# Seven half-width products per pair of feature tiles in a two-layer FFN behind delta-rule attention

## The chip, the cores and the metric

One core of a Trainium2 chip runs the whole program. The time is the device time of one launch in microseconds (us), as the median of several executions. PE is TensorE, DVE VectorE, ACT ScalarE, SP SyncE, which issues the DMAs.

## What is computed

Attention by the delta rule over 4 batches, 8 heads, 768 positions of 48 numbers, then two feed-forward layers over the 3072 tokens of 384 numbers, all in float32:

```
k_n = k / (norm(k) + 1e-06)
for t in range(S):                       # state: 48x48 for each batch and head
    y[:, :, t] = einsum('bhd,bhde->bhe', q[:, :, t], state)
    v_old = einsum('bhde,bhd->bhe', state, k_n[:, :, t])
    state = state + beta_t * einsum('bhd,bhe->bhde', k_n[:, :, t], v_t - v_old)
x = y.transpose(0, 2, 1, 3).reshape(3072, 384)
h = x @ moe_w_in                         # 384 -> 2048
x = maximum(0.01 * h, h) @ moe_w_out     # 2048 -> 384
h = x @ moe2_w_in
out = (h - tanh(h)) @ moe2_w_out
```

## The kernel before

**Tiling.** The positions are cut into 12 chunks n of 64; with four batches a chunk is 256 tokens. Two chunks make one of six pairs u in the attention (`keys`, `grams`, `inverses`, `merges`, then for each chunk `queries`, `products`, `states`, `outputs`). `to_xa` scales a chunk's attention output and turns it, and makes of it the input of the first layer, i = 0; `to_xb` does the same between the first layer and the second, i = 1.

**The layers.** Each float32 product is made of three products of float16: of a high half and a low half of either operand, all but low by low. The 2048 features are 16 tiles in 8 pairs. `h_part` makes a pair's hidden values: 18 products with a block of the first weight (WI) as the stationary operand and 256 columns of x moving, into one bank of ps_h. ACT applies the function (tile sx), ACT copies the high half in float16 (g) and DVE subtracts it for the low half (g again; "g<-sx,g"). `o_part` then takes g as the stationary operand, in blocks of 128 tokens, and the second weight (WO) as the moving one: 12 products of 384 columns per pair, in two banks of ps_o that collect all eight pairs of a chunk. In the program's first moments, PE also measures the two first weights with products of 128 columns ("ps_h<-wi", "ps_o<-wo"). `layer` runs `h_part` for the eight pairs and lets `o_part` follow LAG = 3 pairs later; `layers` gives the order of chunks, two at a time: (0,0) (1,0) (0,1) (1,1) (2,0) and so on.

**Weights.** They arrive as words of float64 in rooms that are free at the time. DVE turns them into float32 (one TENSOR_SCALAR and two SCALAR_TENSOR_TENSOR per two tiles, "wi<-wo,wi"), and they are then scaled and split ("wo<-wo,sw,sx" is the low half of a tile pair of weight 1, the first layer's WO). Weight 3, the second layer's WO, lands in the freed parts of others and in two rooms of x.

**Rooms.** Tiles live in rings: x has 4 rooms, sx 6, g LAG + 1 = 4, kf (keys) 4, kt 3, q, gd and vf 2; in PSUM ps_h and ps_o 2 banks each, ps_a 4, which the attention uses. A tile waits until its room's last reader is done.

**The order.** Nothing is issued as it is written. Every operation is recorded in a `Graph`, with what it reads and writes; a list scheduler then puts all in one order for each engine, by the length of what hangs on an operation plus a number for its stage from the table `BIAS` (some 300 numbers). The engines issue in that order. So all instructions of the trace have the same line, that of the helper: L631 for PE and L634 for the others. Names tell them apart; a name's number is its room.

## Time and profile before

| | |
|---|---|
| median of 3 runs | 954.79 us (954.46 to 954.85) |
| the profiled execution | 953.02 us |
| its span in the trace | 951.3 us |
| PE busy | 898.3 us (94%), 13194 products |
| weight loads (PEld), beside it | 684.2 us (72%) |
| DVE busy | 596.4 us (63%), 1334 instructions |
| ACT busy | 492.2 us (52%), 1193 instructions |
| first products (ps_h, 256 columns) | 3456, 403.7 us of busy time |
| second products (ps_o, 384 columns) | 2304, 400.3 us of busy time |

How to read it: 1.7 us of the profiled execution's time lie outside its span. Busy times are shares of one execution; records of products run into each other, so the mean of one tells less than the distance from start to start in a row of them.

### The profile page before, as it was taken

How to read it: one execution, taken by the hardware profiler on the slowest of the kernel's cores; microseconds unless marked ns; L12 is line 12 of the kernel's file. 1: busy time of each engine (PE TensorE's matmuls, PEld its weight loads, DVE VectorE, ACT ScalarE, POOL GpSimd, SP SyncE). 2: the span in 40 equal slices, each digit the busy share in tenths (PEclk: the TensorE clock that was granted, in tenths of full speed). 3: DMA queues.
4: the chain of work that ended last, by engine and by line, in shares of the span. 5: the costliest groups of instructions: out<-in, count | busy, mean ns of one | idle time of the engine just before them, and what ended most of it. 6: DMA issues, size and time to landing. Idle time of an engine off the chain costs nothing.

```text
span 951.3 us, 29839 instructions
## 1 busy us (share of the span) xinstructions
PE 898.3 (94%) x13194; PEld 684.2 (72%) x13194; DVE 596.4 (63%) x1334; ACT 492.2 (52%) x1193; POOL 4.9 (1%) x22
## 2 busy tenths in 40 slices
PE   3087999999999999999999999999999999999997
PEld 3056877777778778777877777777777777777775
DVE  7999999996984337983598353266943344312432
ACT  5266957976735435735564654354334543434432
POOL 2000000000000000000000000000000000000000
PEclk9587899999999999999999999999999999999999
DMA  9964535643230302222122150031200010000000
GB/s 350 400 209 125 177 99 167 151 133 60 69 60 11 70 22 58 81 45 31 41 58 53 41 94 4 17 57 36 57 1 19 2 36 18 18 18 17 18 17 18
DMA packets 82498, 70.32 MB, mean 74 GB/s; under 512 B 57536, under 2 KB 68800, under 8 KB 82368
## 3 DMA queue, kind: packets, MB, share of 16 engines
q1 hardware_dynamic: 82368, 68.41, 27.1%
q8 instruction: 103, 1.69, 0.7%
q14 instruction: 27, 0.22, 0.1%
HBM read 44.14 MB, written 4.72 MB: 51 GB/s over the span
## 4 chain that ended last, share of the span: by engine, by line
PE 84%; DVE 10%; ACT 3%; DMA 1%; issue 1%; SPq 1%; ACTq 0%; DVEq 0%
PE ps_h L631 38%; PE ps_o L631 38%; PE ps_a L631 8%; DVE wo L634 2%; DVE wi L634 2%; DVE xi L634 2%; DVE gd L634 2%; ACT sx L634 1%; DMA kf<-in_k_dram 1%; SPq L634 1%; ACT jk L634 0%; ACT XW L634 0%; DVE sx L634 0%; ACT gd L634 0%; DVE p L634 0%
## 5 line engine op out<-in xcount | busy, mean ns | idle before, releaser
L631 PE MATMUL ps_h<-x,wi 128*128 128x256 f16 x3456 | 403.7, 273 | 0.3 <-DVE sx L634 0.3
L631 PE MATMUL ps_o<-wo,g 128*128 128x384 f16 x2304 | 400.3, 326 | 0.0
L631 PEld LDWEIGHTS <-wi 128*128 128x128 f16 (+1 forms) x3504 | 340.2, 98 | 77.5 <-DVE wi L634 22.9
L631 PEld LDWEIGHTS <-g 128*128 128x128 f16 x2304 | 222.5, 98 | 133.0 <-DVE g L634 0.2
L634 ACT ACTIVATE g<-sx 128x512 f16<-128x512 f32 x192 | 120.4, 628 | 97.3 <-DVE sx L634 50.0
L634 DVE TENSOR_TENSOR g<-sx,g 128x512 f16<-128x512 f32 x96 | 66.2, 690 | 108.7 <-ACT g L634 108.4
L634 ACT ACTIVATE sx<-ps_h 128x512 f32<-128x512 f32 x96 | 56.9, 595 | 136.6 <-PE ps_h L631 112.3
L634 DVE SCALAR_TENSOR_TENSOR g<-sx,g 128x512 f16<-128x512 f32 x96 | 66.2, 690 | 63.3 <-ACT g L634 62.9
L634 DVE SCALAR_TENSOR_TENSOR sx<-sx,kap,ps_h 128x512 f32<-128x512 f32 x96 | 71.4, 744 | 54.0 <-ACT sx L634 53.8
L634 ACT ACTIVATE sx<-ps_h,kap 128x512 f32<-128x512 f32 x96 | 65.3, 680 | 33.5 <-PE ps_h L631 21.0
L634 DVE TENSOR_TENSOR gd<-xi 128x30 f32<-128x30 f32 (+9 forms) x180 | 59.6, 331 | 2.6
L634 DVE TENSOR_TENSOR xi<-xi,gd 128x30 f32<-128x30 f32 (+9 forms) x180 | 59.7, 332 | 2.3
L634 ACT ACTIVATE jk<-kf 128x48 bf16<-128x48 f32 x160 | 38.3, 239 | 20.3 <-DMA kf<-in_k_dram 17.0
L634 ACT ACTIVATE sx<-x,sxs 128x384 f16<-128x384 f32 (+1 forms) x36 | 25.5, 715 | 13.6 <-DVE sxs L634 11.3
L634 ACT ACTIVATE gd<-ps_a 32x256 f32<-32x256 f32 (+1 forms) x72 | 23.6, 372 | 15.5 <-PE ps_a L631 15.0
L634 DVE SCALAR_TENSOR_TENSOR wi<-wo,wi 128x768 int32<-128x768 int32 x32 | 30.3, 956 | 0.0
L634 ACT ACTIVATION_READ_ACCUMULATOR jk<-kf 128x1 f32 x160 | 30.0, 188 | 0.0
L634 DVE SCALAR_TENSOR_TENSOR sx<-x,sxs,sx 128x384 f16<-128x384 f32 (+1 forms) x36 | 26.9, 749 | 4.2 <-ACT sx L634 4.1
L631 PE MATMUL ps_h<-wi 128*128 128x128 bf16 x48 | 4.6, 284 | 22.7 <-DVE wi L634 22.7
L634 DVE TENSOR_SCALAR sx<-ps_o,kap 128x384 f32<-128x384 f32 x12 | 7.4, 616 | 29.7 <-PE ps_o L631 29.7
L634 ACT ACTIVATE sx<-x 128x384 bf16<-128x384 f32 (+1 forms) x36 | 22.3, 621 | 6.2 <-DVE x L634 3.8
L634 ACT ACTIVATE x<-ps_o,sxs 128x384 f32<-128x384 f32 x23 | 12.6, 579 | 21.4 <-PE ps_o L631 21.3
(129 smaller groups left out, 742.1 us busy)
## 6 DMA issues: line engine op xcount, KB each, us to landing
wo<-in_w_in_dram SPq DMA_DIRECT2D x32, 384.0 KB, 7.9
q<-in_q_dram SPq DMA_DIRECT2D x12, 512.0 KB, 4.2
wi<-in_w_out_dram SPq DMA_DIRECT2D x14, 384.0 KB, 7.7
kf<-in_k_dram SPq DMA_DIRECT2D x12, 384.0 KB, 3.6
vf<-in_v_dram SPq DMA_DIRECT2D x12, 384.0 KB, 3.4
out_dram<-sx SPq DMA_DIRECT2D x48, 96.0 KB, 2.2
x<-in_w_out_dram SPq DMA_DIRECT2D x10, 384.0 KB, 4.3
b<-in_beta_dram SPq DMA_DIRECT2D x6, 512.0 KB, 4.8
```

Of the source, the lines that this page charges most:

```text
L631: self.eng["pe"].matmul(out=o.real(), lhsT=lhsT.real(), rhs=rhs.real(), start=start, stop=stop)
L634: getattr(self.eng[n.on], op)(**{k: v.real() if isinstance(v, View) else v for k, v in kw.items()})
```

## The change

For the chunks from the fifth on (`STRA = 4`), the first layer's second product is made of seven products per pair of feature tiles where a two-by-two scheme has eight: the two halves of the tokens and the two tiles of the pair make a 2x2 array of blocks of g, and the two tiles and the two halves of the output columns a 2x2 array of blocks of WO. The seven products take single blocks or sums and differences of blocks, and each still is three products of float16: 21 products of 192 columns in place of 12 of 384. They collect in four PSUM banks, two of ps_o and two of ps_a, over the chunk's eight pairs.

What comes with it:
- `h_part` makes seven blocks of g in float16 halves in place of four: three more sums on DVE, one more copy on ACT and one more subtraction on DVE, one more room of sx. A room of g grows from 512 to 896.
- `to_xb` gathers a chunk's output from the four banks with four ACT copies and eight DVE steps of 128x3x64, where there were two copies.
- `kept_sums` and `differences` prepare the sums of blocks of the weight, once, ahead of chunk 4. They lie in one room each of q, gd, kt, kf and vf and in a fixed tile, so that these rings have one room less from then on. Blocks of WO are overwritten with differences, after which only the new scheme can use them.
- `layers` takes the first layer of the first four chunks in a row, then their second layer, then pairs as before.
- Weight 3 lands in two rooms of the keys (kf) at u = 2, and no longer in rooms of x.
- The scale of weights 0 and 1 is 2**14 in place of 2**15, so that sums have room.
- `BIAS` is a new table for all stages, so the order on every engine is new. Lines move by seven: L638 for PE, L641 for the others.

```diff
@@ -30,9 +30,11 @@
 def layers(n):
-    out = []
-    for u in range(n // 2):
-        out += [(2 * u, 0), (2 * u + 1, 0), (2 * u, 1), (2 * u + 1, 1)]
+    out, c = [], 0
+    while c < n:
+        w = 2 if c else FIRST
+        out += [(c + j, i) for i in range(2) for j in range(w)]
+        c += w
@@ -55,95 +57,100 @@
 TURNS = 2
+STRA = 4
+LAG = 3
+FIRST = 4
+W3_AT = 2
+WS = (("q", 2, 1), ("gd", 2, 1), ("kt", 2, 1), ("kf", 2, 0), ("vf", 0, 4), ("", 0, 1))
 BIAS = {
-    ('consts', 0): 156.13, ('dma', 'b', 0): 45.42, ('dma', 'b', 1): -53.35, ('dma', 'grams', 10): 13.82,
...
+    ('consts', 0): -120.49, ('diffs', 0): 58.69, ('diffs', 1): 84.59, ('diffs', 2): 88.56,
...
@@ -667,7 +674,6 @@
     NP = NF // 2
-    LAG = 3
@@ -683,7 +689,7 @@
     s_r = ring("sx", SROOMS, 512, short=True)
-    g_r = ring("g", LAG + 1, 512)
+    g_r = ring("g", LAG + 1, 512 if STRA >= NS else 896)
@@ -914,7 +920,7 @@
             dve("tensor_reduce", out=acc[:, 0:1], in_=diag, axis=AX.X, op=ALU.add)
-        pow2_scale(s_, norm_sum(acc, 1 if trace else NF), 2 ** 15)
+        pow2_scale(s_, norm_sum(acc, 1 if trace else NF), 2 ** (15 if i > 1 or STRA >= NS else 14))
@@ -1048,6 +1054,10 @@
                 turn(land[c_].rearrange("p (m i) -> p m i", m=GM), KH[:, c_].rearrange("p m g d -> p (m g d)"))
+                if c_ == 0:
+                    g_.claim(g_.nodes[-1], kt)
+                    if n % 2 == 0 and STRA < NS:
+                        g_.claim(g_.nodes[-1], gd_t[n // 2])
@@ -1074,7 +1084,7 @@
             for t in (Gd, raw_t.get(n // 2)):
-                if t is not None:
+                if t is not None and not (n in K_DMA and STRA < NS):
@@ -1366,6 +1376,57 @@
+    WH = WO[0].rearrange("p f c (t h e) -> p f c h t e", t=KT, h=2)
+    HD2 = DM // 2
+    R, G = [], []
+
+    def te(v):
+        return v.rearrange("p (t e) -> p t e", t=KT)
+
+    def fte(v):
+        return v.rearrange("p f (t e) -> p f t e", t=KT)
+
+    def pair_sum(outs, shape, a, b, op, view):
+
+        s, l = (g_.tile(s_r, shape, F32) for c in range(2))
+        tt(view(s), a[1], b[1], op)
+        g_.claim(g_.nodes[-1], l)
+        for part, o in outs:
+            copy(o[1], part(s))
+        tt(view(l), a[0], b[0], op)
+        tt(l, l, s, ALU.add)
+        for part, o in outs:
+            tt(o[0], part(l), o[1], ALU.subtract)
+
+    def kept_sums():
+        for r, pairs, n in WS:
+            w = 4 * pairs * HD2 + 2 * n * HD2
+            t = g_.tile(dict(q=q_r, gd=gd_r, kt=kt_r, vf=vf_r, kf=kf_r, x=x_r)[r], [128, w], F16) if r else fixed(f"ws{n}", [128, w], F16)
+            for c in range(pairs):
+                R.append(t[:, 4 * HD2 * c:4 * HD2 * c + 4 * HD2].rearrange("p (c f e) -> p c f e", c=2, f=2))
+            for c in range(n):
+                o = 4 * pairs * HD2 + 2 * c * HD2
+                G.append(t[:, o:o + 2 * HD2].rearrange("p (c e) -> p c e", c=2))
+        for p in range(NP):
+            g_.stage = "sums", p // 2
+            f = slice(2 * p, 2 * p + 2)
+            pair_sum([(fte, [fte(R[p][:, c]) for c in range(2)])], [128, 2, HD2], [WH[:, f, c, 0] for c in range(2)],
+                     [WH[:, f, c, 1] for c in range(2)], ALU.add, fte)
+            pair_sum([(te, [te(G[p][:, c]) for c in range(2)])], [128, HD2], [WH[:, 2 * p, c, 0] for c in range(2)],
+                     [WH[:, 2 * p + 1, c, 1] for c in range(2)], ALU.add, te)
+
+    def differences():
+        def half_of(h):
+            return lambda v: v.rearrange("p (t h e) -> p h t e", t=KT, h=2)[:, h]
+
+        for p in range(NP):
+            g_.stage = "diffs", p // 2
+            pair_sum([(half_of(h), [WH[:, 2 * p + 1 - h, c, h] for c in range(2)]) for h in range(2)], [128, DM],
+                     [WO[0][:, 2 * p, c] for c in range(2)], [WO[0][:, 2 * p + 1, c] for c in range(2)], ALU.subtract,
+                     lambda v: v)
+
+
+
@@ -1433,14 +1494,29 @@
         x = g_.tile(x_r, [128, KT * N], F32)
-        for k in range(HB2):
-            cp(rows_of(x)[:, k], po[k][:, 0:DM].rearrange("p (t f) -> p t f", t=KT), sx[:, 2 + k:3 + k])
+        if n < STRA:
+            for k in range(HB2):
+                cp(rows_of(x)[:, k], po[k][:, 0:DM].rearrange("p (t f) -> p t f", t=KT), sx[:, 2 + k:3 + k])
+        else:
+            xr = x.rearrange("p (t k h e) -> p k h t e", t=KT, k=HB2, h=2)
+
+            def gather(k, h, m, *rest):
+                o, sc = xr[:, k, h], sx[:, 2 + k:3 + k]
+                copy(o, product(po, m), sc)
+                for m, op in rest:
+                    stt(o, product(po, m), sc, o, ALU.mult, op)
+
+            gather(0, 0, 4, (2, ALU.subtract))
+            gather(1, 0, 4, (5, ALU.add), (1, ALU.subtract), (7, ALU.add))
+            gather(0, 1, 2, (6, ALU.add), (1, ALU.subtract), (3, ALU.add))
+            gather(1, 1, 3, (5, ALU.add))
         g_.stage = f"h_part{i}", n
+        seven = i == 0 and n >= STRA
@@ -1451,7 +1527,7 @@
         sx = g_.tile(s_r, [128, 2 * N], F32)
-        g = g_.tile(g_r, [128, 2, 2 * N], F16)
+        g = g_.tile(g_r, [128, 2, 7, 128] if seven else [128, 2, 2 * N], F16)
@@ -1459,7 +1535,18 @@
             stt(sx, sx, kap[:, 1:2], ps, ALU.mult, ALU.add)
-        if i == 0:
+        if seven:
+            rs = g_.tile(s_r, [128, 4, 128], F32)
+            g_.claim(node, rs)
+            sq = sx.rearrange("p (j o m) -> p j o m", j=2, o=2)
+            tt(rs[:, 0:2], sq[:, 0], sq[:, 1], ALU.add)
+            tt(rs[:, 2:4], sq[:, :, 1], sq[:, :, 0], ALU.subtract)
+            tt(sq[:, 1, 1], sq[:, 0, 1], sq[:, 1, 0], ALU.add)
+            sq = sx.rearrange("p (q m) -> p q m", q=4)
+            for a, b, src in ((0, 3, sq[:, 1:4]), (3, 7, rs)):
+                copy(g[:, 0, a:b], src)
+                tt(g[:, 1, a:b], src, g[:, 0, a:b], ALU.subtract)
+        elif i == 0:
@@ -1480,6 +1567,29 @@
             g_.ffn(node)
+
+    SEVEN = {4: (0, 0, 1), 2: (0, 1, 3), 1: (1, 0, 2), 5: (1, 1, 4), 3: (2, 0, 0), 6: (2, 1, 5), 7: (3, 0, 6)}
+
+    def product(po, m):
+        b, c, _ = SEVEN[m]
+        return te(po[b][:, c * HD2:c * HD2 + HD2])
+
+    def o_seven(n, po, g, p):
+        g_.stage = "o_part0", n
+
+        e, o = 2 * p, 2 * p + 1
+        w = {1: lambda c: te(G[p][:, c]), 2: lambda c: WH[:, e, c, 0], 3: lambda c: WH[:, e, c, 1],
+             4: lambda c: WH[:, o, c, 0], 5: lambda c: WH[:, o, c, 1], 6: lambda c: te(R[p][:, c, 0]),
+             7: lambda c: te(R[p][:, c, 1])}
+        for m, (b_, c_, q_) in SEVEN.items():
+            if c_ == 0:
+                g_.cut()
+            for n, (a, b) in enumerate(((0, 0), (0, 1), (1, 0))):
+                node = mm(product(po, m), g[:, b, q_], w[m](1 - a), p == 0 and c_ == 0 and n == 0,
+                          p == NP - 1 and n == 2 and (c_ == 1 or m == 7))
+            if c_ or m == 7:
+                g_.ffn(node)
+
@@ -1501,9 +1611,14 @@
             po += [g_.tile(ps_o, [128, 512], F32) for o in range(2)]
+            if i == 0 and n >= STRA:
+                po += [g_.tile(ps_a, [128, 512], F32) for o in range(2)]
             out_scale(kap)
-        o_part(n, i, po, g, p)
+        if i == 0 and n >= STRA:
+            o_seven(n, po, g, p)
+        else:
+            o_part(n, i, po, g, p)
@@ -1552,9 +1667,12 @@
     weight(2, w2_in, WI2[1], (wo[1] * 2)[0:NF])
-    xw = [words(g_.tile(x_r, [128, 2 * DM], F32))[0] for _ in range(2)]
-    weight(3, w2_out, WO[1], (wo[1][nh // 2:] * 2)[0:NF // 2] + xw * (NF // 4))
     for u in range(NU):
+        if u == W3_AT:
+            xw = [words(g_.tile(kf_r if u else x_r, [128, 2 * DM], F32))[0] for _ in range(2)]
+            weight(3, w2_out, WO[1], (wo[1][nh // 2:] * 2)[0:NF // 2] + xw * (NF // 4))
+        if 2 * u == STRA:
+            kept_sums()
@@ -1573,6 +1691,8 @@
     for n, i in layers(NS):
+        if n == STRA and i == 0:
+            differences()
```

The table's numbers tell nothing to the eye; the orders that come of them do. The first place is DVE around the input of chunk 0: the second "sx<-x,sxs,sx" makes the low half of it, "xi" and "gd" are steps of the solving in `inverses`, "wi" is a conversion of weight 2, and "wo" a scaling of weight 1. Before:

```order
L634 SCALAR_TENSOR_TENSOR wi_130<-wo_132,wi_130 128x768
L634 COPY x_62<-ps_a_99 128x3x128
L634 SCALAR_TENSOR_TENSOR sx_66<-x_61,sxs_113,sx_65 128x3x128
L634 COPY u_87<-ps_a_98 128x384
L634 TENSOR_TENSOR xi_90<-xi_90,gd_89 128x26x5
L634 TENSOR_TENSOR gd_89<-xi_90 128x25x6
L634 SCALAR_TENSOR_TENSOR sx_66<-x_61,sxs_113,sx_65 128x3x128
```

After:

```order
L641 COPY x_62<-ps_a_96 128x3x128
L641 TENSOR_TENSOR xi_90<-xi_90,gd_89 128x22x9
L641 SCALAR_TENSOR_TENSOR sx_65<-x_61,sxs_113,sx_70 128x3x128
L641 TENSOR_TENSOR gd_89<-xi_90 128x21x10
L641 SCALAR_TENSOR_TENSOR wo_131<-wo_131,sw,sx_69 128x2x384
L641 SCALAR_TENSOR_TENSOR sx_65<-x_61,sxs_113,sx_70 128x3x128
L641 TENSOR_TENSOR xi_90<-xi_90,gd_89 128x21x10
```

The solving of the second pair of chunks stands four steps further on at the same point (22x9 and 21x10 where 26x5 and 25x6 stood), and a scaling of weight 1 stands between the two halves; five more of these scalings stand ahead of it, where before there was none.

The second place is the end of chunk 4's first layer. Before, ACT empties its two banks of ps_o between the pairs' own steps ("sx<-ps_h" and "g<-sx" are those of the next chunk's pairs):

```order
L634 ACTIVATE g_74<-sx_68 128x512
L634 ACTIVATE sx_66<-ps_h_92 128x512
L634 ACTIVATE g_73<-sx_66 128x512
L634 ACTIVATE sx_66<-ps_h_93 128x512
L634 ACTIVATE x_62<-ps_o_95,sxs_113 128x3x128
L634 ACTIVATE g_71<-sx_66 128x512
L634 ACTIVATE x_62<-ps_o_94,sxs_113 128x3x128
L634 ACTIVATE sx_68,ab_100<-x_62 128x768
```

After, ACT makes four copies, and DVE has five of the eight gathering steps ("x_63<-...,x_63") within twelve instructions; the steps of 128x256 and 128x128 and the last two subtractions into g are those of chunk 5's pairs:

```order
L641 SCALAR_TENSOR_TENSOR x_63<-ps_o_94,sxs_116,x_63 128x3x64
L641 TENSOR_TENSOR sx_67<-sx_70 128x256
L641 TENSOR_TENSOR xi_90<-xi_90,gd_88 128x16x15
L641 SCALAR_TENSOR_TENSOR x_63<-ps_o_95,sxs_116,x_63 128x3x64
L641 TENSOR_TENSOR sx_70<-sx_70 128x128
L641 SCALAR_TENSOR_TENSOR x_63<-ps_o_95,sxs_116,x_63 128x3x64
L641 TENSOR_TENSOR g_73<-sx_67,g_73 128x512
L641 SCALAR_TENSOR_TENSOR x_63<-ps_a_98,sxs_116,x_63 128x3x64
L641 TENSOR_TENSOR g_73<-sx_70,g_73 128x384
L641 TENSOR_TENSOR sx_66<-sx_65 128x256
L641 SCALAR_TENSOR_TENSOR x_63<-ps_a_96,sxs_116,x_63 128x3x64
L641 TENSOR_TENSOR sx_66<-sx_65 128x256
```

What DVE had not done there at all before now stands between the steps that PE's next products need, and the copies of ACT alone no longer free the banks.

## Rows read from the trace of the kernel before

**Rows 1.** The page's 40 slices of 23.8 us: busy tenths, and TensorE's granted clock
```profile
PE   3087999999999999999999999999999999999997
DVE  7999999996984337983598353266943344312432
PEclk9587899999999999999999999999999999999999
```

**Rows 2.** Stretches: length, then busy us of PE, PEld, DVE, ACT, POOL; TensorE's clock
```profile
0.00:105.00 105.00, 58.16 (x1491) 46.87 (x1494) 97.77 (x229) 59.90 (x197) 4.89 (x22) 0.75 0.74 260
105.00:200.00 95.00, 94.30 (x1505) 72.56 (x1501) 93.25 (x195) 73.50 (x163) 0.00 (x0) 0.99 0.54 149
200.00:390.00 190.00, 189.72 (x2825) 143.98 (x2823) 124.33 (x289) 104.52 (x277) 0.00 (x0) 1.00 0.24 54
390.00:946.00 556.00, 555.98 (x7387) 420.80 (x7384) 280.45 (x623) 253.96 (x557) 0.00 (x0) 1.00 0.16 33
```

**Rows 3.** Waits of PE from 111 us on: total us, times, longest
```profile
PE ps_h L631 <- DVE sx L634: 0.3, 1, 0.3
```

**Rows 4.** The chain that ended last, in order of time: start, length, what
```profile
308.25 11.70 PE ps_o L631 x72
785.05 5.89 PE ps_h L631 x54
```

**Rows 5.** PE's timeline, products of 128 columns: start, length, count
```profile
63.62 0.85 PE L631 MATMUL ps_o<-wo 128*128 128x128 bf16 x12
73.15 0.33 PE L631 MATMUL ps_o<-wo 128*128 128x128 bf16 x3
```

**Rows 6.** Weight loads beside the second products: count, busy us, mean ns, idle
```profile
L631 PEld LDWEIGHTS <-g 128*128 128x128 f16 x2304 | 222.5, 98 | 133.0 <-DVE g L634 0.2
```

**Rows 7.** PE's timeline where the first layer's products begin
```profile
103.58 1.96 PE L631 MATMUL ps_a<-u,p 64*64 64x48 f32 x64 [0.59 <-ACT x L634]
105.47 3.87 PE L631 MATMUL ps_h<-x,wi 128*128 128x256 f16 x27
109.85 1.16 PE L631 MATMUL ps_a<-q,kt 48*64 48x64 f32 x64 [0.51 <-DVE x L634]
110.94 3.12 PE L631 MATMUL ps_h<-x,wi 128*128 128x256 f16 x27
```

**Rows 8.** DVE's timeline from chunk 0's second low half to g's first
```profile
99.30 0.62 DVE L634 SCALAR_TENSOR_TENSOR sx<-x,sxs,sx 128x384 f16<-128x384 f32 x1
99.84 0.31 DVE L634 TENSOR_TENSOR xi<-xi,gd 128x150 f32<-128x150 f32 x1
...
102.48 0.69 DVE L634 SCALAR_TENSOR_TENSOR p<-ps_a,maskp 128x512 f32<-128x512 f32 x1
103.08 0.34 DVE L634 TENSOR_TENSOR gd<-xi 128x184 f32<-128x184 f32 x1
...
106.84 1.02 DVE L634 SCALAR_TENSOR_TENSOR wo<-wo,sw,sx 128x768 f16<-128x768 f32 x1
107.77 0.29 DVE L634 TENSOR_TENSOR x<-ps_a,x 128x128 f32<-128x128 f32 x1
...
111.20 0.70 DVE L634 TENSOR_TENSOR g<-sx,g 128x512 f16<-128x512 f32 x1
```

**Rows 9.** ACT's timeline: the last copy of chunk 0's turned input
```profile
103.65 0.59 ACT L634 ACTIVATE x<-ps_a 128x512 f16<-128x512 f32 x1
```

**Rows 10.** DVE's groups by form: count, busy us, mean ns, idle before
```profile
L634 DVE TENSOR_TENSOR gd<-gd,b 128x256 f32<-128x256 f32 x24 | 9.8, 420 | 7.4 <-ACT gd L634 7.4
L634 DVE TENSOR_TENSOR KH<-kf,KH 128x384 f16<-128x384 f32 x16 | 8.8, 552 | 1.8 <-DMA sx<-KH 1.2 <-ACT KH L634 0.3
```

**Rows 11.** The same for ACT: the emptying of ps_o, a copy of 384 columns
```profile
L634 ACT ACTIVATE x<-ps_o,sxs 128x384 f32<-128x384 f32 x23 | 12.6, 579 | 21.4 <-PE ps_o L631 21.3
L634 ACT ACTIVATE KH<-kf 128x384 f16<-128x384 f32 x16 | 8.1, 512 | 3.2 <-DVE kf L634 1.6 <-DMA sx<-KH 1.6
```

**Rows 12.** DMA issues: count, median us to landing
```profile
x<-sx SPq DMA_TRANSPOSE x46, 2.8
```

More of the change, by code (lines that the diff above doesn't have):

```diff
@@ new lines @@
+    ('dma', 'grams', 9): 39.59, ('dma', 'k', 0): 72.62, ('dma', 'k', 1): 365.55, ('dma', 'keys', 10): 121.19,
+    ('dma', 'keys', 11): 10.11, ('dma', 'keys', 2): 37.91, ('dma', 'keys', 3): 19.46,
+    ('dma', 'keys', 4): 27.32, ('dma', 'keys', 5): 91.34, ('dma', 'keys', 6): 16.98,
+    ('dma', 'keys', 7): -58.11, ('dma', 'keys', 8): -18.56, ('dma', 'keys', 9): 25.76,
[3 rows of a table added]
+    ('dma', 'o_part1', 7): 43.6, ('dma', 'o_part1', 8): 24.38, ('dma', 'products', 1): 85.41,
+    ('dma', 'products', 10): 57.07, ('dma', 'products', 11): -1.81, ('dma', 'products', 2): 20.38,
@@ new lines @@
+    ('dma', 'products', 3): -188.98, ('dma', 'products', 4): 6.81, ('dma', 'products', 5): 45.72,
+    ('dma', 'products', 6): -29.17, ('dma', 'products', 7): -9.98, ('dma', 'products', 8): 28.31,
+    ('dma', 'products', 9): -43.35, ('dma', 'queries', 0): 121.48, ('dma', 'queries', 1): 18.85,
+    ('dma', 'queries', 10): -0.3, ('dma', 'queries', 11): 117.17, ('dma', 'queries', 2): 9.58,
+    ('dma', 'queries', 3): 123.68, ('dma', 'queries', 4): -43.93, ('dma', 'queries', 5): -51.66,
+    ('dma', 'queries', 6): 77.93, ('dma', 'queries', 7): -17.3, ('dma', 'queries', 8): -31.11,
@@ new lines @@
+    ('dma', 'weight', 1, 4): 24.38, ('dma', 'weight', 1, 5): 95.84, ('dma', 'weight', 2, 0): -28.38,
+    ('dma', 'weight', 2, 1): -90.63, ('dma', 'weight', 2, 2): -123.53, ('dma', 'weight', 2, 3): 106.15,
+    ('dma', 'weight', 2, 4): 1.34, ('dma', 'weight', 2, 5): 28.42, ('dma', 'weight', 3, 0): -182.07,
+    ('dma', 'weight', 3, 1): -1.38, ('dma', 'weight', 3, 2): 114.96, ('dma', 'weight', 3, 3): 135.09,
+    ('dma', 'weight', 3, 4): 60.05, ('dma', 'weight', 3, 5): 128.16, ('first_keys', 0): -18.79,
@@ new lines @@
+    ('keys', 7): 19.18, ('keys', 9): 162.25, ('merges', 0, 0): -56.64, ('merges', 0, 1): -34.7,
+    ('merges', 1, 0): 64.45, ('merges', 1, 1): -16.85, ('merges', 2): 8.72, ('merges', 3): -14.45,
[6 rows of a table added]
+    ('outputs', 10, 1): 69.04, ('outputs', 11, 1): 121.49, ('outputs', 2, 1): -12.33, ('outputs', 3, 1): 38.41,
+    ('outputs', 4, 1): -27.42, ('outputs', 5, 1): -95.49, ('outputs', 6, 1): 96.47, ('outputs', 7, 1): -0.24,
+    ('outputs', 8, 1): -7.5, ('outputs', 9, 1): -19.71, ('products', 1): 161.62, ('products', 10): -2.27,
@@ new lines @@
+    ('products', 11): -35.4, ('products', 2): -1.23, ('products', 3): -17.92, ('products', 5): -20.76,
+    ('products', 6): -50.67, ('products', 7): -25.21, ('products', 8): 13.53, ('products', 9): 35.32,
+    ('states', 0, 1): -32.46, ('states', 0, 2): 46.07, ('states', 1): 57.08, ('states', 1, 1): 92.97,
+    ('states', 1, 2): -7.36, ('states', 10): -16.85, ('states', 10, 1): 20.58, ('states', 10, 2): 57.66,
+    ('states', 11): 82.15, ('states', 11, 1): 4.81, ('states', 2): 79.92, ('states', 2, 1): 49.05,
@@ L147 @@
+    ('weight', 2, 2): 31.91, ('weight', 2, 3): 166.16, ('weight', 2, 4): 70.16, ('weight', 2, 5): 23.56,
+    ('weight', 3): 57.7, ('weight', 3, 0): 2.94, ('weight', 3, 1): -22.59, ('weight', 3, 2): -62.27,
+    ('weight', 3, 3): -27.57, ('weight', 3, 4): -43.73, ('weight', 3, 5): -85.9,
 }
```

111 lines of the change are left out of this document (41 added, 70 removed), and 29 rows, old and new, of the table BIAS.

## The prediction

> **What bounds the kernel now.** I first read the page's slices [rows 1]. From the sixth slice on TensorE (PE) is at nine tenths or more, at its full granted clock, and in the first five it is not. The sums by stretch say it sharper [rows 2]: of the first 105 us PE works 58.2 and VectorE (DVE) 97.8; from 105 to 946 us PE works 840.0 of 841. Thirdly, the list of waits: from 111 us to the end PE waits once, for 0.3 us [rows 3]. So there are two problems. In the first 105 us the end is set by DVE, which works through conversions, weights and the first attention chunks; after that it is set by the number and length of PE's products, and nothing else. DVE has 1.75 us of idleness from 105 to 200, 65.7 of 190 from 200 to 390, and 275.6 of 556 after that [rows 2]. A change here gains what it takes off PE's products, and loses what it adds ahead of the first one and every wait that it puts between them.
>
> **Part 1, the products themselves.** Two stretches of the chain give the spacing: 72 second products of 384 columns follow each other in 11.70 us, 162.5 ns each; 54 first products of 256 columns in 5.89, 109.1 each [rows 4]. No product of 192 columns is there. The line through the two falls 53.4 ns in 128 columns, so 192 columns come to 109.1 - 26.7 = 82.4. A product of 128 columns, each with a weight load of its own, takes (0.85 - 0.33) / 9 = 57.8 [rows 5]; halfway between that and 109.1 is 83.4. I take 82.5. A pair of feature tiles took 12 products of 384 columns, 1950 ns; now it takes 21 of 192, 1732 ns. That is 217.5 less, in 8 pairs of each of the 8 chunks from the fifth on: 64 x 217.5 = **-13.9 us** (-12.7 with 83.4). A load is recorded with 98 ns [rows 6], more than 82.5, but in rows 5 loads of the same 128 columns kept to a spacing of 57.8, so the record is not the spacing.
>
> The row says 57.8 ns for a product of 128 columns with its own load. The Trainium skill, "TensorE: Matmul & The Clock Gate", section "Back-to-back issue gap", has a rule that speaks against the change: in a stream of loads and products the spacing is set by both, some 81 ns at 128 columns and 131 at 512. By a line through these, an estimate from that page, 192 columns cost 89 and 384 cost 114, so 21 short ones would take 0.50 us more than 12 long ones, 32 us over 64 pairs. By the trace, whose 57.8 and 162.5 both disagree with it, they take 0.22 less.
>
> **Part 2, the start.** The first four chunks' first layers now run in a row, and the planner's table is new; what matters is what stands on DVE ahead of the second low half of chunk 0's input, since PE has no first product without it. That half ends at 99.92 [rows 8]. From the order of the changed kernel I priced every instruction ahead of it by its form's duration: 103.9 us of work against 94.1. The difference: six scalings of weight 1, 0.93 from start to start [rows 8], +5.6; two evictions of chunk 1's products, 0.60 from start to start, +1.2; eight more solving steps at 0.31, +2.5; four copies of 256 columns, near the 0.42 of a form of that size [rows 10], +1.6; smaller ones +1.1; fewer conversions of weight 2 and one copy less, -2.2. In all +9.8, and the half ends near 109.7. Behind it come PE's turns and ACT's copies (the last of them is 0.59 long and ends at 104.24 in the trace [rows 9]); the first h product began at 105.47, behind 64 small attention products that ran from 103.58 [rows 7]. These are no longer in its way: half of them now stand behind it. I put the first h product at 112.0, +6.5. After that, before lost 1.4 us: its first 27 h products took 3.87 instead of 2.95, and then PE stood 0.51 [rows 7]. Half of this I expect to be there again, another half is the half of the attention products, so **+6.8 us** on all that follows; bounds 3 (a planner's order that only looks later, with DVE's idle 7.2 us of the first 105 [rows 2] used up) and 10 (the whole 9.8). The first low half of g, at 111.20 [rows 8], has 111.0 us of work ahead of it instead of 106.1, so it is ready near 116.8; PE has 36 h and 32 small products to do until 116.9. No wait there, with nothing to spare.
>
> **Part 3, what PE's side work costs.** Per pair of the seven, DVE gets two additions or subtractions of 256 columns (0.42 each), one of 128 (0.29 [rows 8]) and one more subtraction of 384 (0.55) [rows 10]: 1.68 us, 108 in all; ACT one more copy of 384 at 0.51 [rows 11], 33 in all. After 390 us DVE would work 280.45 [rows 2] + 107.5 + 18.6 (64 gathering steps at 0.29, below) = 407 of some 544, 75%, and still less than PE. The kept sums and differences (8 pairs; about 29 and 19 us by the same forms) fall between 200 and 390, in the 65.7 idle us; 18 are left. That cover is thin, and if it were gone each us would be one of PE's.
>
> New waits are possible where a chunk's four banks of results are gathered, because four banks are held at once and two of them are attention's. Before, two copies of 0.58 on ACT emptied them [rows 11]; now it is four copies and eight DVE steps of about 0.29, mixed with the pairs' own steps. At the turn from chunk 4 to 5, PE has as cover 64 small products (1.1 us, as the 1.16 of rows 7), 18 h (1.96) and six products of the seven (0.5): 3.6. After the first copy on ACT (0.58) DVE has twelve steps there: five gathers (1.45), three of 256 (1.26), one of 128 (0.29), the subtractions of 512 (0.70 [rows 8]) and 384 (0.55) and a solving step (0.31), 5.1 with the copy. That is up to 1.5. At the turn from 10 to 11 the cover is 18 h only, I take 0.5; the six other turns have 36 to 108 h, and I take 0.3. Sum **+2.3 us**, bounds 0 and 8 (1 us at each of eight turns).
>
> The moved landing of weight 3 (keys' rooms instead of inputs') costs nothing by this reckoning: SyncE's queue has its loads ahead of the keys of the third pair of chunks, and the products that need the weight come near 390 us; without the cover, the keys of chunk 4 are late, which is rival B.
>
> **Sum.** -13.9 + 6.8 + 2.3 = -4.8. The profiled execution took 953.02, 1.7 more than its span; it would become 948.2. The median of before, 954.79, lies 1.8 above it, so 950.0.
>
> **Rivals.** A: the start costs nothing, because DVE's idleness absorbs the 9.8. For it: 7.2 idle us in the first 105. Against: in-order DVE, idle where data from DMAs are missing, not where these steps stand. It gives -13.9 + 2.3 = -11.6, **943.2**.
>
> B: DVE becomes what PE waits for before 250 us; this ends on the other side. The place is the input of chunk 2, whose first layer now comes third, and not fifth. DVE's work ahead of it is 175 us by my prices, against 202; with the shift of the start (6) and the DMA turns (2.8 to landing [rows 12], and a copy) it is ready near 185. PE comes to it at 112 + 62.6 (16 pairs at 3.91: 18 x 0.109 + 12 x 0.1625) + 14.2 of attention = 189. Four us to spare; each us that DVE loses beyond it is one of PE's. At 7.1 us of waits in all the change is worth nothing, and at 15 it would be -13.9 + 6.8 + 15 = +7.9, **962.7**. For it: DVE's 98% from 105 to 200 [rows 2]. Against: those four us.
>
> C: the change doesn't do what it says, since the loads set the pace: 21 x 98 = 2058 ns [rows 6] against 1950, so +6.9 instead of -13.9 and the sum +16: **970.8**. Against: rows 5, and 133 us in which the load queue was idle. The skill's spacing of short products named above would end on this side as well, and further: by that rule +32 instead of -13.9, with the rest of the sum 996.
>
> **How the numbers follow.** Forecast 0.64, A 0.13, B 0.17, C 0.06. The forecast's own bounds are 954.8 - 12.7 + 10 + 8 = 960 above and 954.8 - 13.9 + 3 = 944 below. The range reaches from 942 (A's value) to 960; outside lie C, a third of B and a third of A's spread, together 0.16. A measurement of this kernel tells 0.2% (1.9 us) from no change. Of the forecast's 0.64, 0.49 lie under 952.9, 0.10 within, 0.05 above; A's 0.13 is faster; B's is half same (0.08), half slower (0.09); C is slower. Faster 0.62, same 0.18, slower 0.20.
>
> **What would show it.** Step 1: 84 products of 192 columns (four pairs) in about 6.9 us, in the chain's rows; at 98 or more each, C holds. Step 2: the first h product at 112; at 106 A holds. Step 3: PE's waits after 120 us, 2 to 3 in sum, at the chunk turns and on DVE's x or g; if there is one of over 5 us near 185, B holds. DVE should be busy near 75% after 390 us. The prediction fails above all if the planner's new order puts PE's waits where I have read covers: these are 0 to 4 us thin at four places, and I read them from an order without times.

## The result and the profile after

The changed kernel takes **945.31 us** (median of 4 runs, 945.02 to 947.36) beside 954.62 for the kernel before (954.34 to 954.85): a ratio of 0.9907, with an interval of 0.9890 to 0.9924. It is faster by 9.3 us. The forecast was 950.0, with a range of 942 to 960, so the sign came out as said, and the gain was twice the 4.8 that I had worked out. The profiled execution took 945.02, its span 943.3, 8.0 less than that of before.

The page's slices of the changed kernel, busy tenths of PE and DVE and TensorE's granted clock, to be laid beside [rows 1]:

```profile
PE   3147999999999999999999999999999999999997
DVE  7999999889799934799957789974899964567632
PEclk9568999999999999999999999999999999999999
```

PE's row is the same in both but for the first slices; DVE's is fuller in most slices from the thirteenth on. The sums by stretch (columns as in [rows 2]):

```profile
0.00:105.00 105.00, 50.37 (x1357) 40.09 (x1358) 98.02 (x231) 52.73 (x156) 4.83 (x22) 0.76 0.68 241
105.00:200.00 95.00, 93.45 (x1675) 72.11 (x1674) 89.13 (x194) 64.49 (x159) 0.00 (x0) 1.00 0.46 130
200.00:390.00 190.00, 189.75 (x2512) 144.25 (x2510) 151.18 (x363) 116.58 (x302) 0.00 (x0) 1.00 0.25 60
390.00:946.00 556.00, 548.21 (x8232) 461.02 (x8230) 401.00 (x977) 295.40 (x687) 0.00 (x0) 1.00 0.17 38
```

PE still is what works all the time (the last stretch holds 2.7 us behind the program's end). DVE goes from 280.5 to 401.0 us after 390, from 50% to 73% of what is left of the span. And all waits of PE from 111 us on (compare [rows 3]), in total us, times, longest:

```profile
PE ps_o L638 <- DVE g L641: 1.0, 1, 1.0
PE ps_h L638 <- DVE sx L641: 0.2, 1, 0.2
```

One pair's 21 products of 192 columns, in PE's timeline (start, length, count), with the next pair's products following without a gap:

```profile
421.23 0.41 PE L638 MATMUL ps_a<-wo,g 128*128 128x192 f16 x3
421.47 0.66 PE L638 MATMUL ps_a<-gd,g 128*128 128x192 f16 x6
421.97 0.66 PE L638 MATMUL ps_o<-wo,g 128*128 128x192 f16 x6
422.46 0.41 PE L638 MATMUL ps_o<-vf,g 128*128 128x192 f16 x3
422.71 0.41 PE L638 MATMUL ps_o<-wo,g 128*128 128x192 f16 x3
422.96 0.41 PE L638 MATMUL ps_a<-wo,g 128*128 128x192 f16 x3
```

From 421.23 to 422.96 there are 21 products: 1.73 us, 82.4 ns each. The kept sums are read from the rooms gd and vf here in the place of blocks of WO.

The start, in PE's timeline and then in DVE's (answering to [rows 7] and [rows 8]):

```profile
109.25 0.86 PE L638 MATMUL ps_a<-wi,unit_s 128*128 128x384 f32 x2
...
110.11 4.16 PE L638 MATMUL ps_h<-x,wi 128*128 128x256 f16 x36
114.20 1.15 PE L638 MATMUL ps_a<-u,p 64*64 64x48 f32 x64
115.28 0.34 PE L638 MATMUL ps_o<-wo,g 128*128 128x384 f16 x1
116.62 1.96 PE L638 MATMUL ps_o<-wo,g 128*128 128x384 f16 x11 [1.00 <-DVE g L641]
```

```profile
106.53 0.62 DVE L641 SCALAR_TENSOR_TENSOR sx<-x,sxs,sx 128x384 f16<-128x384 f32 x1 [0.22 <-DMA wi<-sx]
...
107.36 1.01 DVE L641 SCALAR_TENSOR_TENSOR wo<-wo,sw,sx 128x768 f16<-128x768 f32 x1
108.29 0.61 DVE L641 SCALAR_TENSOR_TENSOR sx<-x,sxs,sx 128x384 f16<-128x384 f32 x1
...
115.87 0.69 DVE L641 TENSOR_TENSOR g<-sx,g 128x512 f16<-128x512 f32 x1
```

Chunk 0's second low half ends at 108.90 (99.92 before), the first h product begins at 110.11 (105.47 before).

From the first h product on I summed the distances from one PE record's start to the next one's by kind of product (idle gaps apart), in both traces:

| from the first h product to the last product | before, us | after, us | difference |
|---|---|---|---|
| start of the first h product | 105.47 | 110.11 | +4.6 |
| h, 256 columns, 3456 | 380.9 | 380.3 | -0.6 |
| second products, 384 columns | 377.5 (2303) | 252.4 (1535) | -125.1 |
| second products, 192 columns | none | 111.4 (1344) | +111.4 |
| attention's and other small ones | 80.9 (5932) | 82.5 (5996) | +1.6 |
| idle | 1.0 | 1.3 | +0.3 |

The two rows of second products come to -13.7 together, and the column to -7.8, with rounding the 8.0 of the spans.

### The profile page after: what moved, and what is told of

It is laid out like the page before. It is cut to its first block, busy times and chain, and to the rows that moved or that the text cites. A ratio compares the mean times of both kernels' runs of the same rounds, so it can differ in the third digit from the quotient of the medians.

```text
span 943.3 us, 31629 instructions
## 1 busy us (share of the span) xinstructions
PE 881.8 (93%) x13770; PEld 717.5 (76%) x13770; DVE 739.3 (78%) x1761; ACT 529.2 (56%) x1302; POOL 4.8 (1%) x22
## 4 chain that ended last, share of the span: by engine, by line
PE 84%; DVE 11%; ACT 2%; DMA 2%; issue 1%; DVEq 0%; ACTq 0%
PE ps_h L638 39%; PE ps_o L638 32%; PE ps_a L638 14%; DVE wo L641 2%; DVE wi L641 2%; DVE xi L641 1%; DVE gd L641 1%; DMA kf<-in_w_out_dram 1%; ACT sx L641 1%; DVE g L641 1%; DVE x L641 1%; DMA wi<-sx 0%; DVE XW L641 0%; DVE sx L641 0%; DVE kf L641 0%
## 5 line engine op out<-in xcount | busy, mean ns | idle before, releaser
L638 PE MATMUL ps_h<-x,wi 128*128 128x256 f16 x3456 | 406.1, 273 | 0.2 <-DVE sx L641 0.2
L638 PEld LDWEIGHTS <-wi 128*128 128x128 f16 (+1 forms) x3504 | 339.7, 98 | 72.7 <-DVE wi L641 22.9
L638 PE MATMUL ps_o<-wo,g 128*128 128x384 f16 (+1 forms) x2112 | 337.7, 304 | 1.0 <-DVE g L641 1.0
L638 PEld LDWEIGHTS <-g 128*128 128x128 f16 x2880 | 260.1, 98 | 89.5 <-DVE g L641 1.2
L641 ACT ACTIVATE g<-sx 128x512 f16<-128x512 f32 (+1 forms) x256 | 148.5, 599 | 119.5 <-DVE sx L641 100.0
L641 DVE SCALAR_TENSOR_TENSOR sx<-sx,kap,ps_h 128x512 f32<-128x512 f32 x96 | 71.2, 744 | 62.4 <-ACT sx L641 62.1
L641 ACT ACTIVATE sx<-ps_h,kap 128x512 f32<-128x512 f32 x96 | 65.1, 682 | 83.3 <-PE ps_h L638 59.6
L641 DVE TENSOR_TENSOR g<-sx,g 128x512 f16<-128x512 f32 (+1 forms) x160 | 97.7, 633 | 17.0 <-ACT g L641 16.1
L641 DVE SCALAR_TENSOR_TENSOR g<-sx,g 128x512 f16<-128x512 f32 x96 | 65.9, 688 | 31.7 <-ACT g L641 31.4
L641 ACT ACTIVATE sx<-ps_h 128x512 f32<-128x512 f32 x96 | 56.3, 590 | 45.9 <-PE ps_h L638 32.1
L641 DVE TENSOR_TENSOR sx<-sx 128x256 f32<-128x256 f32 (+1 forms) x192 | 67.2, 375 | 16.7 <-ACT sx L641 15.8
L641 DVE TENSOR_TENSOR gd<-xi 128x30 f32<-128x30 f32 (+9 forms) x180 | 58.9, 327 | 1.7
L641 DVE TENSOR_TENSOR xi<-xi,gd 128x30 f32<-128x30 f32 (+9 forms) x180 | 58.9, 327 | 1.5
L641 ACT ACTIVATE jk<-kf 128x48 bf16<-128x48 f32 x160 | 38.0, 238 | 7.2 <-DMA kf<-in_k_dram 4.3
L641 ACT ACTIVATE sx<-x,sxs 128x384 f16<-128x384 f32 (+1 forms) x36 | 25.7, 715 | 11.7 <-DVE sxs L641 11.2
L641 DVE SCALAR_TENSOR_TENSOR wi<-wo,wi 128x768 int32<-128x768 int32 x32 | 30.0, 952 | 0.0
L641 ACT ACTIVATION_READ_ACCUMULATOR jk<-kf 128x1 f32 x160 | 30.0, 187 | 0.0
L641 DVE SCALAR_TENSOR_TENSOR sx<-x,sxs,sx 128x384 f16<-128x384 f32 (+1 forms) x36 | 26.9, 746 | 2.9 <-ACT sx L641 2.6
L641 ACT ACTIVATE gd<-ps_a 32x256 f32<-32x256 f32 (+1 forms) x72 | 23.5, 372 | 9.8 <-PE ps_a L638 9.3
L638 PE MATMUL ps_a<-ident,kf 64*64 64x64 f32 x256 | 7.4, 312 | 21.8 <-DVE kf L641 21.8
L641 ACT ACTIVATE sx<-x 128x384 bf16<-128x384 f32 (+1 forms) x36 | 22.3, 620 | 8.2 <-DVE x L641 7.9
L638 PE MATMUL ps_a<-wo,g 128*128 128x192 f16 x192 | 26.3, 246 | 0.0
```

The costliest lines, as they stand in the source:

```text
L638: self.eng["pe"].matmul(out=o.real(), lhsT=lhsT.real(), rhs=rhs.real(), start=start, stop=stop)
L641: getattr(self.eng[n.on], op)(**{k: v.real() if isinstance(v, View) else v for k, v in kw.items()})
```

## The experiments

All of them are the changed kernel in its own order, with a few lines at the place where the order is issued, since a changed table would change the whole order. "ONE" is an idle reduction of 256 columns on DVE that nobody reads; what several of them add is counted by DVE's time from start to start. What an experiment costs is told as the difference of its ratio to the kernel before and the changed kernel's 0.9907, times 954.6 us; the intervals of both make that uncertain by some 2 to 3 us. The expectations call the runs e1 (1, below), e2 and e5 (2), e9 (3), e3 and e6 (4), e4 and e7 (5), e8 (6), e6b (7), e10 and e11 (8).

**1. The same order, 12 long products for 21 short ones.** In `o_seven` only the products 4, 1, 3 and 7, one for each bank, are issued, 384 columns wide:

```diff
+                if c_ == 0:
+                    alt.append((po[b_][:, 0:DM], g[:, b, q_], WO[0][:, f[m], 1 - a], ...))
+                node.alt = alt
```

> The changed kernel in its own order, but each pair's 21 products of 192 columns are issued as 12 products of 384 columns into the same four banks (the sums of blocks of g and of the weight are still made, and the output is not the layer's). Theory 1, the gain is the products' length alone: 64 pairs x (1.950 - 1.732) = +13.9 us over the changed kernel's 945.3, so 959.2, with PE's waits unchanged. Rival, the gain is mostly the new order of the whole program: 945 to 950.

961.6 us, ratio 1.0072 (1.0050 to 1.0094), +15.8. In its trace the second products take 377.7 us where the changed kernel's took 363.8 (252.4 + 111.4): +13.9, the forecast's number, and the other 2 to 3 us are its start (first h at 110.94) and 2.0 us more of idle gaps. PE's timeline at the same place (six products take 0.97 us from start to start, 162 ns each):

```profile
422.35 1.14 PE L638 MATMUL ps_a<-wo,g 128*128 128x384 f16 x6
423.32 1.14 PE L638 MATMUL ps_o<-wo,g 128*128 128x384 f16 x6
```

So the gain is in the products' length: with long products and all of the rest of the change, the kernel is slower than before.

**2. Less work for DVE ahead of chunk 0's input.** The low halves of weight 1 that stand there become float16 copies:

```diff
+                if op == "scalar_tensor_tensor" and SIZE[kw["out"].ap.dtype] == 2:
+                    n.calls["dve"] = "tensor_copy", dict(out=kw["out"], in_=kw["in1"])
```

> The changed kernel in its own order, but the low halves of weight 1 that are scaled on VectorE ahead of chunk 0's second low half are not computed: a float16 copy of the high half stands in their place. Each scaling takes 0.93 us from start to start; the copy is estimated between 0.3 and 0.55, so six of them give back 2.3 to 3.8 us ahead of the first h product. Theory, VectorE's queue sets the start and each us there is one of the end: first h product at 106.3 to 107.8 instead of 110.1, the time 941.5 to 943.0. Rival, the start hangs on data that land late (VectorE waited 0.22 us for a DMA just ahead of the low half): first h product at 109 to 110 and the time within 1 us of 945.3.

944.45 us, ratio 0.9893 (0.9872 to 0.9914), -1.3: the 2.3 to 3.8 us did not come in full, and what did lies within the uncertainty. The same kernel once more:

> One look at the kernel of e2_six (float16 copies in place of the six early scalings of weight 1), which came out no faster than the changed kernel, for the place where the 2 to 4 us went. Theory 1: VectorE's queue is shorter, but the halves of chunk 0's input wait for something else (a DMA that frees their room, or the attention chain behind them), so that VectorE idles by what was taken away and the first h product stays at 109 to 110. Theory 2: the first h product does come 2 us earlier, at 108, and PE gives it back in a wait on g or on the weight a few us behind.

945.04 us in its one run, and the first h product at 109.94 (109.28 in the trace of the first time). DVE's timeline shows where the time went; a copy takes 0.26 from start to start where a scaling took 0.93, and then:

```profile
94.43 0.35 DVE L648 COPY wo<-sx 128x768 f16<-128x768 f16 x1
94.69 0.28 DVE L648 TENSOR_TENSOR gd<-xi 128x130 f32<-128x130 f32 x1
97.10 0.56 DVE L648 TENSOR_SCALAR wi<-wo 128x768 int32<-128x768 int32 x1 [2.12 <-DMA wo<-in_w_in_dram]
...
104.09 0.56 DVE L648 SCALAR_TENSOR_TENSOR vf<-ps_a,vf 128x384 f32<-128x384 f32 x1 [0.76 <-PE ps_a L645]
```

DVE waits 2.12 us for a load of weight 2 that lands at 97.1, and 0.76 for an attention product. In the trace of the first time it waits 0.14 for that load, 1.28 for a copy of ACT's and 0.78 for the attention product. So theory 1 held in the main: these stood close behind DVE's queue in the changed kernel, unseen. The gain is not nothing: the second low half ends at 107.39 and 108.13 in the two traces, where ten traces of the unshortened start (last section) have 109.5 in the mean, and the first h product comes at 109.28 and 109.94 for their 110.7. By these traces, 1 to 2 of the 4 us came back at the half and about 1 at the first product.

**3. More work at the same place.** Five ONE ahead of the first low half of chunk 0's input:

> The changed kernel with five idle reductions of 256 columns on VectorE (0.41 us each in e6's and e7's rows, 2.0 us) ahead of the first low half of chunk 0's input. Taking about 4 us of VectorE's work away there (e2, e5) moved the first h product by 0.2 us only, since VectorE then idled 2.1 us for a load of weight 2 and 0.8 for an attention product. Theory, VectorE's queue, that load and the attention chain end together, so less work gives nothing but more work costs in full: first h product 1.6 to 2.0 us later, at about 112, and the time +1.5 to +2. Rival, the start doesn't hang on VectorE at all: +0 to +0.3 us.

948.6 us, ratio 0.9933 (0.9913 to 0.9953), +2.5 for 2.23 us of work. In its timelines (DVE, then PE) the reductions, the waits of PE's turning products on DVE, and what came of them:

```profile
106.33 2.23 DVE L645 TENSOR_REDUCE g<-unit 128x1 f32<-128x256 f16 x5
```

```profile
110.89 0.71 PE L639 MATMUL ps_a<-unit,sx 128*128 128x128 f16 x5 [1.51 <-DVE sx L646]
111.40 1.59 PE L639 MATMUL ps_a<-wi,unit_s 128*128 128x384 f32 x2
...
113.11 4.60 PE L639 MATMUL ps_h<-x,wi 128*128 128x256 f16 x36
```

The second low half ended 1.9 us later than in the changed kernel (110.83) and the first h product came 3.0 later, more than what was added: the way between the two is 2.27 us, where it is 1.21 in all ten traces of the unchanged start. Behind the wait the two products "wi,unit_s" took 1.59 where they took 0.86, and the 36 h 4.60 for 4.16; the stretches say why (length, busy times, then the granted clock, as in [rows 2]):

```profile
108.00:111.00 3.00, 0.83 (x9) 0.53 (x9) 2.97 (x7) 0.73 (x3) 0.00 (x0) 0.95 0.18 61
111.00:114.00 3.00, 3.00 (x13) 1.79 (x13) 3.00 (x7) 2.99 (x6) 0.00 (x0) 0.50 0.48 139
```

After a stretch in which PE worked 0.83 of 3 us the clock was at 0.50, its lower level of 1.2 GHz. Against that, PE's wait of 1.0 for the first g is gone, which paid a part of it back.

**4. The gathering doubled, and half of that.** One ONE behind each of the eight gathering steps of a chunk, and then behind every second:

```diff
+            if n.on == "dve" and n.stage[0] == "to_xb" and n.stage[1] >= STRA and op == "scalar_tensor_tensor" and kw["in0"].psum:
+                self.eng["dve"].tensor_reduce(out=self.spare.real(), in_=self.grid.real(), axis=AX.X, op=ALU.add)
```

> The changed kernel with one idle reduction of 256 columns on VectorE behind each of the eight gathering steps of chunks 4 to 11 (64 in all, about 0.34 us each from start to start, 2.7 us more per gather). Theory of the prediction, the cover at the turns is thin: waits of PE at six of the eight turns, where the last gathering step ends 0.4 to 2 us ahead of the next chunk's products or behind their beginning, 0.5 to 2 us each, +3 to +10 us. Rival, the banks are needed one after another and the gather runs ahead of the last product, so the cover is wide: +0 to +1 us.

962.4 us, ratio 1.0077 (1.0054 to 1.0100), +16.2 for some 21 us of work: a record of ONE is 0.41 us long, but the next instruction begins 0.33 behind its start, and 64 x 0.33 = 21:

```profile
439.60 0.41 DVE L644 TENSOR_REDUCE unit_s<-unit 128x1 f32<-128x256 f16 x1
439.93 0.28 DVE L642 TENSOR_TENSOR sx<-sx 128x128 f32<-128x128 f32 x1
```

> The changed kernel with one idle reduction of 256 columns on VectorE behind every second of the eight gathering steps of chunks 4 to 11 (1.35 us more per gather, 10.8 in all). Doubling it (21.6 us) cost 17 us, 0.8 of what was added. Threshold theory, a gather has some 0.6 us of cover: 8 x (1.35 - 0.6) = +6. Theory of no cover, VectorE is what PE waits for at the turns as soon as anything is added: 0.8 of 10.8, +8.6. Prediction's view of the thin cover with its own sizes (0.4 to 2 us at six turns): +1 to +4.

953.29 us (10 runs), ratio 0.9984 (0.9973 to 0.9995), +7.4 for some 10.5 us (32 of 0.33).

About three quarters comes through in both (the prediction's 1 to 4 us are out; the threshold's 6 and the 8.6 of no cover are both within the measurement's uncertainty of 7.4). In the trace of the half it is many small waits of PE, none over 1 us: 6.5 us of idle gaps from the first h product on, in place of 1.3.

**5. The pairs' side work doubled, and a fifth of that.** One ONE behind each of the five VectorE steps of a pair of the seven, and then behind one of the five:

> The changed kernel with one idle reduction of 256 columns on VectorE behind each of the five subtractions and sums of a pair of the seven (about 0.34 us each, 1.7 us per pair, 108 us in all: the side work of the seven doubled). Theory A, what counts is VectorE's share over the long stretch (401 us busy of 553 after 390 us, with this 509, still under PE): +0 to +3 us. Theory B, cover does not carry over from the second layer's stretches to the first's, since only four rooms of g lie between: per pair PE takes 1.96 + 1.73 = 3.69 us, VectorE some 2.0 + 1.7 = 3.7 and the attention's steps on top, so the first layer's stretches become VectorE's: +10 to +40 us, with waits of PE on g.

1012.55 us, ratio 1.0607 (1.0581 to 1.0634), +66.8 for some 105 us of work (320 of 0.33).

> The changed kernel with one idle reduction of 256 columns on VectorE per pair of the seven (0.34 us, 22 us in all), a fifth of what e4_side added, which cost 67 us of 108. Threshold theory, a pair has some 0.65 us of cover (42 us in all, about the difference of 108 and 67): 0 to +1 us. Proportional theory, no cover in these stretches: 0.62 of 22, +13.

950.89 us (8 runs), ratio 0.9956 (0.9943 to 0.9970), +4.7 for some 21 us (64 of 0.33).

The two theories had 0 to 1 and 13 for the small dose, and it came out between: a fifth comes through of it, and nearly two thirds of the large one. With the large one, the stretch behind 390 us reads

```profile
390.00:1011.00 621.00, 569.99 (x8238) 469.59 (x8235) 497.49 (x1297) 300.56 (x688) 0.00 (x0) 0.98 0.16 35
```

DVE works 497 us there, less than the 548 that PE's products took in the changed kernel and the 570 that they take here; so theory A, which counts by the long stretch, falls. B had the place right (PE's waits on DVE's g come to 17.6 us), but named 10 to 40, and more came. In the same trace the gaps of PE come to 46.6 us in place of 1.3, and the products of 192 columns take 126.9 in place of 111.4, beside a granted clock of 0.98 where it was 1.00.

**6. A late input for chunk 2.** Thirty ONE ahead of the first low half of chunk 2's input, at rival B's place:

> The changed kernel with 30 idle reductions of 256 columns (about 10 us) on VectorE, once, ahead of the low half of chunk 2's input. In the changed kernel's trace that input has landed at 184.1 and PE comes to it at 189.2. Rival B's reckoning, 5.0 us of cover and every us beyond one of PE's: +5 us, with one wait of about 5 us near 189. No-cover theory (VectorE is full from 105 to 200, and g's low halves queue behind): +8 to +10 us, with waits on g before 189. Wide-cover theory: +0 to +1.

959.73 us, ratio 1.0064 (1.0041 to 1.0086), +15.0. The thirty took 13.6 us, not 10. The changed kernel there, in the timelines of DVE, SyncE's queue and PE:

```profile
178.52 0.62 DVE L641 SCALAR_TENSOR_TENSOR sx<-x,sxs,sx 128x384 f16<-128x384 f32 x1
...
179.52 0.42 DVE L641 COPY PM<-ps_a 128x256 f32<-128x256 f32 x1
...
180.49 0.21 PE L638 MATMUL ps_a<-XW,PM 32*32 32x32 f32 x1
...
181.50 2.64 SPq L641 DMA_TRANSPOSE x<-sx  x2
...
189.17 3.00 PE L638 MATMUL ps_h<-x,wi 128*128 128x256 f16 x26
```

And with the thirty, DVE and then PE:

```profile
177.35 13.58 DVE L645 TENSOR_REDUCE unit_s<-unit 128x1 f32<-128x256 f16 x30
...
191.84 0.42 DVE L646 COPY PM<-ps_a 128x256 f32<-128x256 f32 x1
```

```profile
192.31 0.26 PE L639 MATMUL ps_a<-XW,PM 32*32 32x32 f32 x1 [12.75 <-DVE PM L646]
```

The input itself had its 5 us (landed at 184.1, needed at 189.2). But two instructions behind it DVE copies PM for the merging of the second pair of chunks, and PE's queue has a product of it among the layer's second products: that one waited 12.75 of the 13.6 us, and all behind it with it. Cover there: 0.8 us, or 0.55 by the changed kernel's own trace, from the copy's end at 179.94 to that product at 180.49. None of the three theories had this place; in size the one without cover was nearest.

**7. The sums' cover.** One ONE behind each of the 104 VectorE steps of the kept sums and differences:

> The changed kernel with one idle reduction of 256 columns on VectorE (0.41 us) behind each of the 104 VectorE steps of the kept sums and the differences, some 42 us between about 175 and 390, where VectorE was idle for 38.8 us of 190 in the changed kernel. Theory of the prediction, cover is counted by the stretch: the idle time takes nearly all of it, +3 to +6 us. Theory after e4, e7 and e8, cover is what stands behind the next step that PE's queue waits for, 1 us or less at a place: a quarter to a half of it comes through, +10 to +20 us, in waits of PE on g, x and the attention's steps.

972.22 us, ratio 1.0175 (1.0156 to 1.0194), +25.6 for some 34 us of work (104 of 0.33). The stretch and PE's longest waits:

```profile
200.00:390.00 190.00, 177.16 (x2077) 130.98 (x2076) 160.09 (x401) 106.35 (x266) 0.00 (x0) 0.97 0.20 48
```

```profile
PE ps_h L638 <- ACT sx L642: 9.0, 4, 4.0
PE ps_h L638 <- DVE sx L642: 4.5, 7, 1.6
```

DVE is still idle for 30 of 190 us in that stretch, and PE waits all the same: 19.2 us of gaps in all, and h products that took 386.8 us in place of 380.3, since the clock is lower behind the longer waits (0.97 for the stretch). Counting cover by the stretch, as the prediction did, fails here; even more came through, three quarters of what was added, than the second theory's 10 to 20.

**8. PE's last wait.** The first low half of g goes ahead of a conversion and two solving steps:

```diff
+        order.remove(low)
+        order.insert(high + 1, low)
```

> The changed kernel with one VectorE instruction moved three places up: the first low half of g, which ended at 116.55 while PE waited 1.0 us for it (PE's only wait of over 0.3 us after the first h product), now stands ahead of a conversion of weight 2 (0.95 us) and two solving steps. Theory, that wait is the last one to be had: about 1.0 us off, 944.3 against the unchanged order's 945.3, too little to be told from noise by the medians alone but to be seen in the trace as a gone wait. Rival, the conversion that now comes later keeps ACT and with it the next bank of h back: a new wait of up to 1 us a few us behind, the time unchanged.

946.88 us, ratio 0.9910 (0.9892 to 0.9928): no gain. And the changed kernel once more:

> The changed kernel itself once more, beside e10 on the same chip. All theories: within 1 us of 945.3. What it tells is how far the first h product and the median move from call to call with nothing changed: in the kernels with the same instructions up to that point it came between 109.3 and 111.8.

945.79 us, ratio 0.9907 (0.9891 to 0.9924). In the trace of the first of the two, the wait for g is gone and another, on ACT, stands behind it, as the rival had it; that the conversion is what delays ACT is not shown. The gaps of PE come to 1.7 us in the one and 1.9 in the other:

```profile
116.12 2.12 PE L642 MATMUL ps_o<-wo,g 128*128 128x384 f16 x12
118.59 3.11 PE L642 MATMUL ps_h<-x,wi 128*128 128x256 f16 x27 [0.34 <-ACT sx L645]
```

So no version faster than the changed kernel came of this.

## Why the prediction was right, and where it was not

**Part 1, the products: right in mechanism and size.** 82.5 ns was forecast for 192 columns and 82.9 measured over all 1344; -13.9 was forecast, -13.7 measured in the sum and +13.9 in experiment 1. The rule of spacing from the Trainium skill's "TensorE: Matmul & The Clock Gate", section "Back-to-back issue gap", from which the estimate of a loss of 32 us was made, doesn't hold for these two widths: 82.9 and 164.4 ns in the trace stand where the estimate had 89 and 114. Rival C, loads at 98 ns that set the pace, is out by the same row.

**Part 2, the start: right in mechanism, too large by 0.9.** The second low half was forecast for 109.7 and ended at 108.90; in ten traces of this same start it ends between 108.06 and 110.61, 109.5 in the mean, so this step was right and the 0.8 is that one execution's. The first h product was forecast for 112.0, and came at 110.11: 1.2 us behind the half and not 2.3, and 1.21 in all ten. The step that failed is what I took for this way between from the kernel before, where ACT's three copies stood among other work and PE had idled. Nor did the slow first h products return. In before the granted clock was 0.59 in the two us from 105.4 on, behind PE's waits of 1.01 and 0.59:

```profile
105.40:107.40 2.00, 2.00 (x19) 1.47 (x12) 2.00 (x5) 2.00 (x5) 0.00 (x0) 0.59 0.88 326
```

In the changed kernel PE has products for weight 0's low halves ("wi,unit_s") and the attention to do there, waits 0.3 us at most between 99 and the first h product, and the granted clock is 1.00 from 100 to 122. The wait for the first g, forecast as none "with nothing to spare", was 1.0, since PE came 1.3 us earlier and DVE's half only 0.2 (116.56 for 116.8). In the table above the start is +4.6 + 1.6 (64 small products that moved behind the first h) - 0.6 + 0.3 = 5.9 for the 6.8 of the forecast. Experiments 2 and 3 confirm what it hangs on, but not alike in both directions: 2.23 us more on DVE move the half by 1.9 and the first h product by 3.0, and 4 us less give back about 1 there, since a load, a copy of ACT's and the attention chain end close behind. This the trace of the changed kernel alone does not show: DVE waits 0.22 us there. How far the start of the kernel before moves from one execution to the next is not known, since there is one trace of it.

**Part 3, the waits at the turns: +2.3 forecast, none measured.** PE's only other wait of the list above, 0.2 us at 368.2, lies ahead of all turns. The step that failed is the price of the first turn, chunk 4 to 5. I set twelve DVE steps against the PE work between the last product of one chunk and the first of the next, as though the gather could only begin behind the former and had to end ahead of the latter. In the changed kernel the gather begins before and ends behind:

```profile
437.91 0.42 DVE L641 SCALAR_TENSOR_TENSOR x<-ps_o,sxs,x 128x192 f32<-128x192 f32 x1 [0.28 <-ACT x L641]
...
444.98 0.41 DVE L641 SCALAR_TENSOR_TENSOR x<-ps_o,sxs,x 128x192 f32<-128x192 f32 x1
```

```profile
439.96 0.66 PE L638 MATMUL ps_a<-kf,g 128*128 128x192 f16 x6
...
443.62 0.66 PE L638 MATMUL ps_o<-wo,g 128*128 128x192 f16 x6
```

The four banks are done one after another and needed one after another: the first step comes 2.7 us ahead of the last product's end (440.6), the last one 1.4 us behind the beginning of the next chunk's. The size of a gathering step does not explain it: I had taken 0.29, and it is 0.33 from start to start (437.91 to 438.24), so by my reckoning the wait would have been longer. That the cover is thin was right, and experiment 4 shows it (three quarters of what is added comes through), but nothing of it is paid until something is added.

DVE's share after 390 us was forecast as 407 us of 544 (75%) and is 401 of 553 (73%). Why that is no problem is not the share: the large dose of experiment 5 costs 67 us and experiment 7 costs 26, with DVE still under PE in the sum.

**The rivals.** A (a start for nothing) is out: 5.9 us in these two traces. B had the right time of its input (185 forecast, 184.1; PE there at 189, 189.2) and the right idea that DVE is full, but the wrong place: the product that waits first is one of the attention, two DVE instructions on, with 0.8 us of cover where I saw 4 (experiment 6).

**The sum.** Of the 4.7 us between 950.0 and 945.31, 2.3 are the waits, 0.9 is the start, and 1.5 has nothing to do with the kernel: I took the median to lie 1.8 above the profiled execution, as in before, and it lies 0.3 above it. By spans the forecast was -4.8 and the result -8.0.

What stays open: how much of the start's 5.9 us is the order of layers and how much the new table. The one can't be undone without the other, since a table made for one order gives another one by chance, and it was not tried.

## What to carry to other kernels

When one engine works without a gap, a change that shortens its instructions gains their number times the difference of their spacing, and the spacing of a width that the trace lacks could here be had from the line through its neighbours (82.5 ns for 82.9). The idle share of the engine beside it says little about cover: look, at each place where work is added, for the next instruction of the bound engine's queue that depends on the delayed engine, even one of another stage, and measure the distance of these two. And a queue that sets a start can have others right behind it, as here; price an addition in full, but a removal only down to the next of them.
